# A planner's order of work replaced by a listed one, in a fused attention and MLP kernel

## Chip, core and metric

The kernel runs on one core of a Trainium2 chip. The metric is the device time of one launch in microseconds. Five engines work side by side, each through its own list of instructions in order: TensorE (PE in the profile: matrix products; PEld its weight loads), VectorE (DVE), ScalarE (ACT), GpSimd (POOL) and SyncE (SP), which here issues nearly all DMAs. An instruction whose inputs or whose buffer are not ready holds up all that stand behind it on its engine.

## What is computed

```python
def _attn_ref(q, k, v, g_norm):                      # q, k, v: (8, 8, 576, 64)
    kv = np.einsum('bhsd,bhse->bhde', k, v)
    out = np.einsum('bhsd,bhde->bhse', q, kv)
    rms = np.sqrt(np.mean(out * out, axis=-1, keepdims=True) + 1e-06)
    return (out / rms * g_norm).astype(np.float32)

def _moe_ref(x, w_in, w_out):                        # (4608, 512) (512, 2048) (2048, 512)
    h = x @ w_in
    g = np.maximum(h, 0.0) + np.log1p(np.exp(-np.abs(h)))
    return (g @ w_out).astype(np.float32)
```

Between the two, the attention's output (batch, head, position, 64) is laid out as x, 4608 tokens by 512. Linear attention makes a 64 by 64 matrix kv of each head of a batch; a row of q times it, normed, is a row of x. Then comes an MLP with a softplus. The weights arrive as 64-bit floats, so each is turned to 32 bits on the chip.

## The kernel before

**Precision.** The products are made with 32-bit operands that TensorE rounds. To lose nothing, each operand is split in parts: a rounded high part, and the rest (on ScalarE `high`, on VectorE `low` and `less`). A product is then three passes of parts.

**The stages.** x is worked on in tiles of 128 tokens, 36 in all, tile t from batch t*128 // 576. Before any MLP work:
- `weight(j)`: weight piece j (even: w_in, odd: w_out, of chunk c = j // 2 of 128 hidden units) is loaded (L423, 512 KB), squared for an overflow check on ScalarE (L434, L451), and turned to 32 bits by six operations of VectorE (L438, L442, L447, L455, L460, L464). `split_weight` splits it (L501 or L503, L508 or L511, L514, then on TensorE L525 and L526, L529).
- `kv_of(b)`: k and v of a batch come in four pairs p of 256 KB loads (L685) and a remainder (L683); 16 small products each (L696) add up kv, and ScalarE copies it out (L704).
- `rows(t)`: q of tile t is loaded (L766), transposed on TensorE (L776) and copied by ScalarE (L783); multiplied with kv (L720); squared (L793, ScalarE), summed (L724, VectorE), inverse root (L727 and L728, GpSimd, 2.0 us together), multiplied (L732, VectorE), and transposed (L738). From batch 2 on, q comes by `load_q` and VectorE transposes it (L751).
- `split(t)`: x of the tile is split, L640 on ScalarE, L643 and L646 on VectorE. A block is three tiles, 384 tokens. Its x is also stored (L802, L803) for later use.

**The MLP** has two forms. The first blocks go through `step(s)`: block n times chunk c, `mm1` (12 products, L864), softplus (L886), split (L888 on ScalarE, L875 and L879 on VectorE), and three times `mm2` (3 products each, L871). The first steps are 0 to 3 for block 0 with chunks 0 to 3, then 4 to 7 for block 1, and so on; step 0 needs the three tiles of block 0 split, and weight 0. Later work (`wide_step`, L1066 to L1137) takes 512 tokens at a time and saves products by sums and differences of quarters; it makes up two thirds of the time.

**What sets the order.** None of the functions issues anything: each calls `plan.add(engine, ns, run, after, pos, take, give, ...)`, which appends a task, and `plan.slot(ring)`, which names a buffer to be taken from a ring of buffers. `Plan.order()` then plays the tasks through, with their estimated times `ns`, a model of the DMA's backlog and the positions `pos`, and picks at each point the task that can start first. It also gives each slot its place in its ring. Wherever TensorE would idle for 400 ns by this play (until step 6), it puts in a filler `warm` (L1232): a product of the identity with itself, whose result nobody reads. The result is one list of tasks, and the engines' instructions are issued in its order.

```python
    plan.spare = ("h", warm, 400, mm1s[6][1])
    for t in plan.order():
        t.run()
```

Slots bind engines together: the loads of k and v go through four buffers (`e`), so the load of k's pair 2 has to wait until TensorE has used pair 0. The buffers of weight loads are one for w_in (`raw`) and one for w_out (`rawb`).

## Time and profile before

| | |
|---|---|
| Median of 3 runs | 859.08 us (858.3 to 861.02) |
| The profiled execution | 858.19 us, of it the span of the trace 856.4 us |
| TensorE busy | 843.0 us (98%) |
| VectorE, ScalarE, GpSimd busy | 704.1, 520.6, 76.6 us |
| Fillers (L1232) | 52, from 1.61 to 74.0 us |
| Step 0's first product (L864) | at 44.09 us |
| First output product (L871) | at 58.26 us |
| HBM read, written | 112.98 MB, 52.95 MB |

The span is the time from the first to the last instruction of the trace, and times in the text are counted from its start. In the tables of stretches each engine has its busy time and, in brackets, how many instructions started there; in the timelines a line has the start, the length, the engine, the line of the kernel, and in square brackets how long the engine was idle before and what ended that. A TensorE group's length reaches to the end of its last product's pipeline, so the next group can start before it.

### The profile page before, as it was taken

What the parts mean: (1) busy time and instruction counts of PE and PEld (TensorE: products, weight loads), DVE (VectorE), ACT (ScalarE), POOL (GpSimd) and SP (SyncE); (2) the same over time, 40 slices, a digit from 0 to 9 for tenths busy, and PEclk for the clock granted to TensorE, in tenths of its full rate; (3) what the DMA queues carried; (4) which work ended last, traced back from release to release, by engine and by line L of the source; (5) the groups of instructions that cost most, each with busy time, mean ns of one, the idle gap of its engine ahead of it and who ended that gap; (6) DMA issues with size and microseconds to landing.
All of it is one profiled execution on the core that took longest, in us unless ns stands there. A gap on an engine that the chain in (4) does not pass through costs nothing.

```text
span 856.4 us, 17075 instructions
## 1 busy us (share of the span) xinstructions
PE 843.0 (98%) x6464; PEld 754.1 (88%) x6464; DVE 704.1 (82%) x995; ACT 520.6 (61%) x980; POOL 76.6 (9%) x79
## 2 busy tenths in 40 slices
PE   8899999999999999999999999999999999999998
PEld 5578898999898999999999999998999899999996
DVE  7888898888788889798898788878788766788873
ACT  6766665446344567766667665655868555566654
POOL 0351223111113300000000000000000000000000
PEclk9999999999999999999999999999999999999999
DMA  9998997778884755436644546645364753777864
GB/s 283 297 233 212 261 273 232 185 245 218 214 188 119 194 160 185 142 110 207 210 156 154 180 151 206 195 158 181 124 197 138 234 168 102 240 237 246 249 189 131
DMA packets 239778, 167.07 MB, mean 195 GB/s; under 512 B 106320, under 2 KB 198736, under 8 KB 239696
## 3 DMA queue, kind: packets, MB, share of 16 engines
q1 hardware_dynamic: 239392, 165.86, 65.9%
q8 instruction: 50, 0.82, 0.4%
q14 instruction: 32, 0.26, 0.1%
q10 hardware_dynamic: 304, 0.13, 0.1%
HBM read 112.98 MB, written 52.95 MB: 194 GB/s over the span
## 4 chain that ended last, share of the span: by engine, by line
PE 94%; ACT 1%; DVE 1%; DMA 1%; issue 1%; POOL 0%; SPq 0%; POOLq 0%; DVEq 0%; ACTq 0%
PE banks L1137 31%; PE banks L1066 28%; PE banks L871 16%; PE banks L864 15%; PE banks L720 2%; PE banks L696 2%; DMA loads<-in_k_dram 1%; PE banks L738 0%; PE banks L1232 0%; PE banks L776 0%; DVE units L643 0%; DVE half L732 0%; DVE roots L724 0%; POOL roots L728 0%; ACT w L783 0%
## 5 line engine op out<-in xcount | busy, mean ns | idle before, releaser
L1137 PE MATMUL banks<-pieces,gv 128*128 128x512 f32 x768 | 236.8, 390 | 0.0
L1137 PE MATMUL banks<-pieces,g_False 128*128 128x512 f32 x384 | 149.4, 389 | 0.0
L1137 PEld LDWEIGHTS banks<-pieces,gv 128*128 128x128 f32 x768 | 132.5, 188 | 17.2 <-DVE banks L910 0.2
L864 PE MATMUL banks<-units,pieces 128*128 128x384 f32 x768 | 144.8, 337 | 0.0
L871 PE MATMUL banks<-pieces,gv 128*128 128x512 f32 x576 | 143.3, 393 | 0.0
L864 PEld LDWEIGHTS banks<-units,pieces 128*128 128x128 f32 x768 | 134.7, 188 | 4.5
L871 PEld LDWEIGHTS banks<-pieces,gv 128*128 128x128 f32 x576 | 106.2, 188 | 19.0
L1066 PEld LDWEIGHTS banks<-units,pieces 128*128 128x128 f32 x840 | 111.0, 188 | 6.5 <-ACT banks L1112 0.4
L1066 PE MATMUL banks<-units,pieces 128*128 128x256 f32 x840 | 115.2, 280 | 0.0
L886 ACT ACTIVATE half<-banks 128x384 f32<-128x384 f32 x64 | 31.4, 491 | 94.0 <-PE banks L864 90.7
L1127 DVE TENSOR_TENSOR gv<-g_True,gv 128x1024 fp32r<-128x1024 f32 x47 | 57.5, 1223 | 35.6 <-ACT gv L1124 35.5
L1137 PEld LDWEIGHTS banks<-pieces,g_False 128*128 128x128 f32 x384 | 72.1, 188 | 15.0
L1066 PEld LDWEIGHTS banks<-units,w 128*128 128x128 f32 x504 | 66.7, 188 | 3.7 <-ACT banks L1112 0.2
L1066 PE MATMUL banks<-units,w 128*128 128x256 f32 x504 | 69.6, 280 | 0.0
L728 POOL TENSOR_TENSOR roots<-roots,half 128x8 f32<-128x8 f32 x36 | 62.3, 1731 | 3.0
L1130 DVE SCALAR_TENSOR_TENSOR g_False<-gv 128x1024 fp32r<-128x1024 f32 x47 | 57.6, 1225 | 1.5
L1029 DVE TENSOR_TENSOR units<-loads,units 128x1024 fp32r<-128x1024 f32 x42 | 51.2, 1219 | 6.0 <-ACT units L1026 5.9
L1094 ACT ACTIVATE g_True<-banks 128x256 f32<-128x256 f32 x96 | 36.7, 384 | 30.6 <-PE banks L1066 29.9
L1116 DVE TENSOR_TENSOR g_True<-banks,g_True 128x512 f32<-128x512 f32 x48 | 33.1, 690 | 25.8 <-PE banks L1066 19.8
L931 ACT ACTIVATE m<-banks 128x512 f32<-128x512 f32 x72 | 42.1, 595 | 18.2 <-PE banks L1137 12.5
L1032 DVE SCALAR_TENSOR_TENSOR units<-units 128x1024 fp32r<-128x1024 f32 x42 | 51.4, 1224 | 1.7
L1026 ACT ACTIVATE units<-loads 128x1024 fp32r<-128x1024 f32 x42 | 44.3, 1056 | 12.4 <-PE banks L1066 10.1
(115 smaller groups left out, 1248.7 us busy)
## 6 DMA issues: line engine op xcount, KB each, us to landing
loads<-x SPq DMA_DIRECT2D x180, 128.0 KB, 2.7
part<-m SPq DMA_DIRECT2D x72, 256.0 KB, 3.1
m<-part SPq DMA_DIRECT2D x72, 256.0 KB, 3.4
loads<-form SPq DMA_DIRECT2D x45, 256.0 KB, 3.2
form<-loads SPq DMA_DIRECT2D x36, 256.0 KB, 3.0
raw<-in_moe_w_in_dram SPq DMA_DIRECT2D x16, 512.0 KB, 4.7
loads<-in_k_dram SPq DMA_DIRECT2D x32, 256.0 KB, 4.0
loads<-in_v_dram SPq DMA_DIRECT2D x32, 256.0 KB, 4.5
```

What stands on the lines that cost most here:

```text
L728: nc.gpsimd.tensor_tensor(out=r.tile, in0=r.tile, in1=half, op=ALU.pow)
L864: nc.tensor.matmul(from_the_end(hp, w), lhsT=w_in.tile[:, i, kd * P:(kd + 1) * P], rhs=from_the_end(xv.tile[:, i, kd], w), start=(m == 0), ...
L871: nc.tensor.matmul(mine[i].tile, lhsT=gv.tile[:, m, i * P:(i + 1) * P], rhs=w_out.tile[:, m], start=(c == cs[0] and m == 0), stop=(c == cs ...
L931: a = add("ACT", 690 if ph == LAST else 600, lambda: nc.scalar.activation(new(ot, [P, d_model]), bank.tile, func=AF.Copy, scale=scale if p ...
L1026: nc.scalar.activation(part_of(0, F32R), xl.tile if m > 1 else xl.tile[:, 0], func=AF.Copy, scale=DOWN)
L1029: nc.vector.tensor_tensor(out=part_of(1, F32R), in0=xl.tile if m > 1 else xl.tile[:, 0], in1=part_of(0), op=ALU.subtract)
L1032: nc.vector.scalar_tensor_tensor(out=part_of(2, F32R), in0=part_of(1), scalar=-RADIX, in1=part_of(0), op0=ALU.mult, op1=ALU.add)
L1066: nc.tensor.matmul(from_the_end(place(q), (16, 8)[kd]), lhsT=w[:, m, at:at + P], rhs=from_the_end(dst.tile[:, m, v, kd] if u < 6 else dst. ...
L1094: nc.scalar.activation(dst, src, func=AF.Softplus, scale=1.0 + E)
L1127: nc.vector.tensor_tensor(out=gvt(1, F32R), in0=gt(), in1=gvt(0), op=ALU.subtract)
L1130: nc.vector.scalar_tensor_tensor(out=gt(F32R), in0=gvt(1), scalar=-RADIX, in1=gvt(0), op0=ALU.mult, op1=ALU.add)
L1137: nc.tensor.matmul(from_the_end(mine[i].tile, P), lhsT=(gvt(m, F32R) if m < 2 else gt(F32R))[:, c, i * P:(i + 1) * P], rhs=from_the_end(ou ...
```

## The change

`Plan.order()` no longer plays anything through. It takes two constants: `TURNS`, the order of all tasks, and `HOMES`, the place of each slot in its ring. In `TURNS` a number n from 0 is the n-th task that was added, -1 and -2 are fillers in the first or second bank of ring `h`.

```diff
+TURNS = [
+    -1, -2, -1, -2, -1, -2, -1, -2, 0, 373, 386, 14, 370, 371, 428, 387, -1, -2, -1, -2, -1, -2, -1, -2, -1, -2, -1, 1, 2, 3, 4, 374, 6, 5, 16, 7, 15, 17,
+    28, 388, 372, -2, 18, 376, 429, -1, -2, -1, 382, 20, 21, 430, 8, 19, 375, -2, -1, -2, -1, -2, -1, -2, -1, -2, -1, -2, -1, -2, -1, -2, -1, -2, -1, -2,
...
+]
+
+HOMES = (
...
+)
...
     def slot(self, ring):
-        return Slot(ring)
+        self.slots.append(Slot(ring))
+        return self.slots[-1]
...
-    def order(self):
...
+    def order(self, turns, homes):
+        for s, at in zip(self.slots, homes):
+            s.place = int(at, 36)
+        ring, run = self.spare
+        done = []
+        for n in turns:
+            if n >= 0:
+                done.append(self.tasks[n])
+                continue
+            s = Slot(ring)
+            s.place = -1 - n
+            done.append(Task("PE", 0, lambda s=s: run(s), [], 0.0, [s], [s], 0))
+        assert len(homes) == len(self.slots) and sorted(n for n in turns if n >= 0) == list(range(len(self.tasks)))
+        return done
...
-    plan.spare = ("h", warm, 400, mm1s[6][1])
-    for t in plan.order():
+    plan.spare = ("h", warm)
+    for t in plan.order(TURNS, HOMES):
         t.run()
```

Read against the old order, the list holds the same 3795 tasks. `HOMES` gives every slot that is used the place that it had. The engines' lists differ in their first part only, and are the same from there on:

| engine | tasks in the part that differs, of all | which starts, in the old trace, until |
|---|---|---|
| SP | 73 of 737 | 72 us |
| PE | 234 of 1164, old 207 of 1137: 79 fillers, old 52 | 155 us |
| ACT | 185 of 948 | 162 us |
| DVE | 237 of 989 | 160 us |
| POOL | none of 36 | |

The beginnings, old and new (kv p: the products of pair p of batch 0; W j: weight piece j; q t: q of tile t; r: the remainder of k or v):

| engine | old | new |
|---|---|---|
| SP | W0, k 0, k r, W1, v 0, v 1, k 1, q 0, v r, q 3, W2, k 2, v 2, v 3, W3, k 3, q 1, q 4, k 0 of batch 1, q 4, W4, ... | W0, k 1, q 0, W1, k 0, v 0, q 3, v 1, W2, k 2, k r, k 3, W3, v 3, v 2, v r, q 1, q 4, q 4, W4, ... |
| PE | 13 fillers, kv 0, 2 fillers, kv 1, 1, q 0 transposed, W0 split, 1, q 3, 5, W1 split, 1, kv 2, 6, kv 3, kv r, q 1, W2 split, rows of tile 0, ... | 8 fillers, q 0 transposed, 11 fillers, kv 0, 1, q 3, 3, kv 1, 20 fillers, W0 split, 3, kv 2, kv 3, kv r, 2, rows of tile 0, q 1, W1 split, ... |
| PE, from step 0 on | step 0, x 4, rows 6, W5, q 7, x 5, step 1, kv 0 and 1 of batch 2, rows 7, step 2, x 6, 1 filler, rows 8, W6, L871 of step 0, ... | step 0, rows 6, x 4, step 1, q 7, 1 filler, W5, x 5, rows 7, one L871 of step 0, step 2, x 6, kv 0 and 1 of batch 2, rows 8, two L871 of step 0, ... |

On VectorE the six operations of a weight and the two of a split stood mostly one behind the other; in the new list an operation on something else often stands between two that depend on each other. L438 of W1 stands before L460 of W0, and L508 of W2 right behind L464 of W2. On ScalarE, step 0's L888 stands right behind its L886 (old: seven tasks stand between); L501 of W0 and L434 of W2 stand before L503 of W1; and the first kv copy (L704) stands behind L514 of W0, L451 and L501 of W2 and L434 of W3.

More of the change, by code (lines that the diff above doesn't have):

```diff
@@ L61 @@
 class Plan:
-    HANDOVER = {"PE": 250, "ACT": 120, "DVE": 120, "POOL": 150, "SP": 0}
-    READY = {"PE": 2500, "ACT": 2500, "DVE": 4000, "POOL": 2500, "SP": 700}
-    SWITCH = {("all", "rows"): 90, ("all", "kv"): 90, ("rows", "all"): 250, ("kv", "all"): 250, ("rows", "kv"): 140, ("kv", "rows"): 140}
-    TOGETHER, PATIENCE = 1, 0.0
-    LANDING, FILLED = 3500, 60000
-    KEEP = 4
-    BEGIN = 4000
-    SOON = 150
     def __init__(self, rings, heirs):
@@ L79, in __init__ @@
         self.spare = None
+        self.slots = []
     def slot(self, ring):
-        return Slot(ring)
+        self.slots.append(Slot(ring))
+        return self.slots[-1]
     def add(self, engine, ns, run, after=(), pos=0.0, take=(), give=(), size=0, behind=None, follows=None, kind="all"):
```

117 lines of the change are left out of this document (11 added, 106 removed), and 146 rows, old and new, of the table TURNS.

## The prediction

> **What bounds the kernel now.** I read the page's busy shares and its forty slices first, to find the stages; then the busy time of each engine in stretches of the opening; then the timelines of TensorE (PE), VectorE (DVE) and SyncE (SP) there.
>
> ```profile
> PE 843.0 (98%) x6464; PEld 754.1 (88%) x6464; DVE 704.1 (82%) x995; ACT 520.6 (61%) x980; POOL 76.6 (9%) x79
> ...
> PE   8899999999999999999999999999999999999998
> ```
>
> TensorE is busy 98% of the span, and the slices show where it is not: the first two (43 us) and the last. All that the change moves on TensorE lies before the third tile product of batch 5 (L696) at 155.27 us; from there its list is the old one. So whatever happens, the end moves by as much as that point does.
>
> ```profile
> core 0: us, PE busy (x) PEld busy (x) DVE busy (x) ACT busy (x) POOL busy (x), PEclk, DMA share, GB/s
> 5.00:10.00 5.00, 4.09 (x32) 2.54 (x33) 4.71 (x9) 2.62 (x5) 0.37 (x1) 1.00 1.10 336
> 30.00:40.00 10.00, 8.01 (x149) 5.96 (x143) 8.54 (x15) 8.24 (x17) 4.16 (x4) 1.00 1.01 284
> 40.00:50.00 10.00, 9.16 (x138) 7.57 (x137) 9.29 (x16) 6.34 (x13) 4.11 (x4) 1.00 0.99 236
> 60.00:80.00 20.00, 19.89 (x253) 16.45 (x252) 17.45 (x32) 11.76 (x24) 6.28 (x6) 1.00 0.85 214
> 80.00:155.00 75.00, 75.00 (x746) 67.21 (x745) 67.47 (x117) 44.55 (x87) 19.41 (x18) 1.00 0.89 246
> ```
>
> Until some 40 us the DMA engines are full (share 1.0 to 1.1), VectorE is busy 85 to 94%, and part of TensorE's 80% is filler (L1232: a product nobody reads). After 60 us TensorE has no idle time left. The timeline of TensorE shows the opening:
>
> ```profile
> 1.61 5.92 PE L1232 MATMUL banks<-ident_r 128*128 128x512 f32 x13 [1.61 <-DVE ident_r L1192]
> 8.43 0.69 PE L696 MATMUL banks<-loads 128*64 128x64 f32 x16 [0.91 <-DMA loads<-in_v_dram]
> ...
> 11.18 0.63 PE L776 MATMUL banks<-ident_r,early 128*128 128x128 f32 x4 [0.30 <-DMA early<-in_q_dram]
> ...
> 42.59 1.66 PE L1232 MATMUL banks<-ident_r 128*128 128x512 f32 x6
> 44.09 2.25 PE L864 MATMUL banks<-units,pieces 128*128 128x384 f32 x12
> ...
> 57.06 0.69 PE L720 MATMUL banks<-early,w 64*64 64x64 f32 x32 [0.44 <-ACT w L802]
> ```
>
> The point to watch is 44.09 us, where step 0's first product (L864) starts: real work, then fillers, then the step. Before it lie 20.8 us of real work (34 tasks), some 15 us of fillers and the idle time. After it, up to 155.27, TensorE idles 1.43 us in five gaps and runs 2 fillers.
>
> **The change, part by part.** Durations are from one execution, 858.19 us with a span of 856.4; the sum is made against 858.19. The median of three is 859.08, so 0.9 is added at the end.
>
> *Nothing added or removed but fillers.* The 3795 tasks are the same, and so is the place of every buffer. TensorE gets 79 fillers instead of 52. GpSimd's order is untouched.
>
> *Fillers.* They cost 0.43 us each in the first stretch (2.20, 2.63, 3.06 us and on) and 0.235 after 9 us. A filler is free where TensorE would wait, and paid in full where it would not. In the list 8 come first, 70 between the transposition of q's tile 0 (L776) and step 0, one after. I set the path of TensorE up to step 0 by the starts in the trace: 10 kv products at 0.57, 9 q transpositions at 0.41, 5 weight splits at 0.6, 6 row products at 0.55, 4 x transpositions at 0.4: 17.3; 70 fillers at 0.235 are 16.4, and the first filler of each of 17 groups costs 0.1 more, 1.7. Together 35.4 us. That transposition can start when q's tile 0 lands. Its load goes from eighth on SP to third. There the trace has a load issued at 2.40 and landed at 6.62; q is twice its size, so I take 6.9. Step 0 thus starts at 42.3 at the earliest, and by half a filler (0.12) of left-over gap in each of 17 groups, 2.0, at 44.3. Old: 44.09.
>
> *VectorE up to step 0.* The last input of step 0 is the third part of tile 2 (L646), started at 43.97. A VectorE operation that reads its neighbour's result starts later than one that doesn't:
>
> ```profile
> 28.29 0.69 DVE L643 TENSOR_TENSOR units<-banks,units 128x512 fp32r<-128x512 f32 x1
> 29.02 0.69 DVE L646 SCALAR_TENSOR_TENSOR units<-units 128x512 fp32r<-128x512 f32 x1
> 29.63 0.68 DVE L732 TENSOR_TENSOR half<-banks,roots 128x512 f32<-128x512 f32 x1
> ```
>
> 0.73 us from start to start where the second reads the first, 0.61 where not. Up to that operation the old order has 26 such neighbours and the new one 15: 11 by 0.12, minus 1.3. Two operations fewer stand before it (0.6 each, minus 1.2; the memset L1179 that comes in costs 0.1). The old waits on the way (0.70, 0.19, 0.48, 0.21, 0.99: 2.6) go. New ones come, by position: the first operation on weight 1 (L438) now stands before weight 0's L460, and its load, which landed at 7.63, has 128 KB more ahead of it (q in place of k's remainder) and lands near 8.0: VectorE idle from 7.16, plus 0.85; the residue of weight 1 (L511) waits for ScalarE, which now does a square of weight 2 (L434) first, plus 0.7; that of weight 2 (L508) stands right behind the sum (L464) that ScalarE must read first, 0.85. So 43.97 - 1.2 + 0.1 - 1.3 - 2.6 + 2.4 = 41.4, with as much again of waits unseen (2.6) 44.0. The two paths give 42.3 to 44.3 and 41.4 to 44.0; step 0 waits for both. I take 43.3, 0.8 us earlier, and keep 42.3 to 46.8 (the upper end from the rival with the clock, below).
>
> On chained operations the Trainium skill (VectorE: DVE Perf Modes, The DRAIN you can't avoid) says the opposite of this row: each operation drains anyway, and one can't gain by how they are chained. By it the 1.3 us would not be there, VectorE's path would read 42.7 to 45.3 and the sum some 0.7 more. The rows decide for 0.12 us a pair.
>
> *SyncE and the loads.* All 73 entries that move are loads and stores of the opening; bytes are the same, and the DMA engines are full there, so what comes forward pushes others back. Weight 2 gains about 1.4 us (14.08 to 12.6), but k's pair 2 (L685) needs the buffer that the first kv product (L696) frees. In the old order that was over at 9.12 and the load left at 10.33 unhindered; in the new one 11 fillers and a transposition stand before that product, it ends near 10.9, and everything behind on SP waits: weight 3 leaves at about 13.7 instead of 12.20 and lands near 18.1, old 17.79. Cost on the path: nothing as long as VectorE reaches weight 3 only at 18.4, as its sum above says; up to 1.9 us if that product is later still. What else goes back has room: weight 6 landed at 33.8 and is first read at 41.6, and the x tiles of the stores (L803) are read again no sooner than 65 us.
>
> *ScalarE.* The rounding of step 0's softplus (L888) stood five microseconds behind the softplus (46.38 to 51.44, with splits of later tiles in between); now it follows at once. The first output product (L871) moves before step 2's first product. Worth nothing by itself, since TensorE has other work; it takes away the reasons to idle later. ScalarE's waits (the kv copy L704 stands behind four of weight operations) are inside the 2.6 above.
>
> *After step 0.* From 44.09 to 155.27 the old order takes 111.2 us. With each task at the smallest start-to-start time that its kind, before its next kind, shows in the trace (2.08 for a first product, 0.68 for an output product, 0.47 to 0.58 for kv and rows), the same tasks need 106.8; the new order, with its other neighbours, 106.7. So 4.4 us are to be had, of which 2.7 before 60 us, 1.3 to 80 us, the rest later. I count the part after 80 us as staying, 1.6, and 0.6 of new waits (the first L871 now stands where VectorE's L879 may be about a microsecond late): minus 2.2. Bounds: 4.4, and plus 2 where each early output product waits.
>
> Sum: 858.2 - 0.8 - 2.2 = 855.2; plus 0.9 for the median: **856.1**.
>
> **The rivals.** *A: as before.* The opening is bound by the loads and by VectorE, both full, and the fillers fix step 0 at 44.3; the 4.4 us come back as other waits. For it: DMA share 1.1; 27 fillers more are 6.3 us that can't be skipped. Against it: VectorE's sum without unseen waits ends at 41.4, and the waits of TensorE behind step 0 are on work that the list now brings forward. 858 to 860.5.
>
> *B: slower, by the clock.* The 13 fillers of before ran at 0.427 us each without a break until 7.5 us; those from 9.05 on at 0.235. So TensorE runs at half speed until it has worked for some six microseconds. The new list has 8, over at 5.03, and then a wait for q until 6.9. If the full clock comes only at about 11.3, the 11 fillers that follow cost 0.19 more each, 2.1, and the kv product 0.4 more; k's pair 2 leaves at 12.7, the DMA engines run dry for some 2 us, weight 3 lands at 19.7. All fillers being fixed, nothing catches it up: step 0 at 44.3 + 2.5 = 46.8. If the gain behind it is then lost too: 858.2 + 2.7 + 0.9 = 861.8. It decides from step 0 at 46.7 with nothing gained behind.
> The Trainium skill (TensorE: Matmul & The Clock Gate, Part 1) has this as a rule: a free-running window of about 3.4 us must be busy throughout. By it 8 cold fillers, 3.42 us, hardly ever fill one, and the clock would come between 10.3 and 13.7. The trace agrees that it takes longer than one window (1.61 to at least 6.9 us), and shows no case with a pause.
>
> *C: all of it.* Step 0 at 42.3, and 4 us gained behind: 852.4 + 0.9 = 853.3. Needs no leftover gaps at all.
>
> **How the numbers follow.** About 0.3%, 2.6 us, is what a measurement of this kernel can tell from no change: faster means below 856.5, slower above 861.7. Forecast (854 to 857.5) 0.45, of which 0.36 below 856.5; A 0.22; B 0.25, of which four fifths beyond 861.7, since a late step 0 and waits behind it come together; C 0.08. Faster 0.44, same 0.36, slower 0.20. The range reaches from C's 853.3 to a little beyond B, 862.5; the forecast's own is 854 to 857.5.
>
> **What would show it.** Right: the first L864 between 42.5 and 44; fillers at 0.235 by 8 us; the last L646 before it started before 43.5; the L888 of step 0 within a microsecond of its L886; the kv product that starts TensorE's common part at 152 to 153 instead of 155.27; idle time of TensorE between step 0 and there below 1 us. Wrong: fillers at 0.427 beyond 9 us; SP idle at L685 between 9 and 13 us and a drop in the DMA share there; the first L864 after 45; a wait of more than 1 us before the first L871. A shift of the end that is not the shift of that kv product would contradict the frame of the whole sum.

## The result, and the profile after

The changed kernel takes **867.42 us** (median of six, 864.99 to 869.77), the kernel before 858.58 us beside it (six, 858.30 to 861.02): a ratio of 1.0096, 95% interval 1.0072 to 1.0119. It is 8.8 us slower; 856.1 was forecast, and the range ended at 862.5. The profiled execution took 869.77 us with a span of 868.0, the slowest of its six, so sums against its trace (11.6 us of span) are some 3 us larger than the medians' 8.8.

Lines are now those of the changed kernel: 60 higher than before, so L924 is the first product (L864), L931 the output product (L871), L756 the kv product (L696), L836 the transposition of q (L776), L1292 the filler (L1232), L483 a weight load (L423), L745 a load of k or v (L685). In the experiments' profiles they are 18 or 19 lower than that.

The page's busy line of TensorE and its forty slices, as they were shown of before:

```profile
PE 853.9 (98%) x6491; PEld 761.4 (88%) x6491; DVE 700.2 (81%) x995; ACT 517.7 (60%) x980; POOL 78.2 (9%) x79
...
PE   7899999999999999999999999999999999999998
```

TensorE is busy 10.9 us longer, 98% of the span as before: the share tells nothing. The stretches do, with the columns of before. First the kernel before from 10 to 20 us, then the changed kernel:

```profile
10.00:20.00 10.00, 8.52 (x93) 6.04 (x90) 8.84 (x16) 7.75 (x15) 0.00 (x0) 1.00 1.09 319
```

```profile
5.00:10.00 5.00, 2.24 (x8) 1.69 (x8) 2.45 (x5) 1.60 (x5) 0.25 (x1) 1.00 0.92 287
10.00:20.00 10.00, 10.00 (x65) 7.48 (x64) 5.45 (x10) 4.25 (x10) 0.00 (x0) 1.00 0.65 187
30.00:40.00 10.00, 7.49 (x125) 5.49 (x124) 8.58 (x16) 6.50 (x14) 3.82 (x4) 1.00 1.04 270
40.00:50.00 10.00, 9.78 (x112) 7.57 (x112) 7.00 (x12) 6.25 (x13) 2.99 (x3) 0.83 0.93 212
60.00:80.00 20.00, 19.86 (x255) 17.15 (x256) 16.73 (x31) 12.87 (x27) 6.87 (x5) 1.00 0.84 238
80.00:155.00 75.00, 73.39 (x778) 62.53 (x777) 62.01 (x110) 41.01 (x84) 19.48 (x18) 1.00 0.85 224
```

Three things differ. From 10 to 20 us the DMA share is 0.65 where before had 1.09: the queue of loads stands still, and VectorE has 5.45 us of work instead of 8.84. From 40 to 50 us the clock is 0.83. And behind 80 us, where TensorE had no idle time at all, it loses 1.6 us. The timeline of TensorE shows the opening:

```profile
1.61 3.78 PE L1292 MATMUL banks<-ident_r 128*128 128x512 f32 x8 [1.61 <-DVE ident_r L1252]
8.15 1.08 PE L836 MATMUL banks<-ident_r,early 128*128 128x128 f32 x4 [2.76 <-DMA early<-in_q_dram]
8.88 5.04 PE L1292 MATMUL banks<-ident_r 128*128 128x512 f32 x11
13.86 0.69 PE L756 MATMUL banks<-loads 128*64 128x64 f32 x16
...
23.23 1.15 PE L756 MATMUL banks<-loads 128*64 128x64 f32 x32 [0.57 <-DMA loads<-in_v_dram]
...
40.22 0.38 PE L798 MATMUL banks<-ident_r,half 128*128 128x128 f32 x2 [2.38 <-issue]
...
41.48 2.93 PE L1292 MATMUL banks<-ident_r 128*128 128x512 f32 x6
...
52.07 2.36 PE L924 MATMUL banks<-units,pieces 128*128 128x384 f32 x12
```

The 11 fillers at 8.88 take 0.46 us each, twice the 0.235 of the full clock (the trace has the full clock from 13.89 on; the column PEclk, which reads 1.00 from 5 to 20 us, does not show this), so the first kv product comes at 13.86 instead of 8.43. Step 0 starts at 52.07, 8.0 us later than before.

To follow a loss through a trace I use one measure below, the **lag**: how much later TensorE has finished a given amount of real work (each product group counted at its usual length, fillers not at all) than in the trace of before. In the new kernel it is 9.5 us at 51 us, falls to 5.7 at 100, rises to 11.1 at 170, and stays within half a microsecond of that. So there are two losses: one in the opening, of which 3.8 us are made up behind step 0, and a second of 5.4 between 105 and 170.

Both show the same picture, a queue in order whose head waits. The queue of loads (SPq) in the opening, and ScalarE there:

```profile
10.37 0.37 SPq L483 DMA_DIRECT2D raw<-in_moe_w_in_dram  x1
14.58 0.37 SPq L745 DMA_DIRECT2D loads<-in_k_dram  x1
...
17.24 0.41 SPq L483 DMA_DIRECT2D g<-in_moe_w_out_dram  x1
```

```profile
9.90 0.57 ACT L843 COPY w<-banks 128x512 f32<-128x512 f32 x1
15.45 0.59 ACT L843 COPY w<-banks 128x512 f32<-128x512 f32 x1 [4.97 <-PE banks L836]
```

The load of k's pair 2 (14.58) waits for the first kv product, so weight 3 (17.24) leaves 5.05 us later than before and lands at 21.4 (17.79). ScalarE idles 4.97 us at a copy of q of tile 3, whose transposition stands behind that same kv product; its work for weights 0 and 1 is queued behind, and VectorE idles from 14.08 to 18.46. Little of this reaches TensorE directly before step 0, though. VectorE comes to weight 3 (L498, `g`) only 1.3 us after it has landed, right behind other work:

```profile
22.10 0.69 DVE L520 SCALAR_TENSOR_TENSOR m<-raw,m 128x512 f32<-128x512 uint32 x1
22.71 0.42 DVE L498 TENSOR_SCALAR m<-g 128x512 uint32<-128x512 uint32 x1
```

TensorE waits 0.57 us for the load of v at 23.23, which stands behind weight 3 in the queue, and 0.25 for VectorE at 36.03; from 8.15 to step 0 it idles 3.3 us in all, 2.38 of them in the gap at 40.22 that nothing in the trace releases ("issue").

The second place, the queue of loads and then ScalarE:

```profile
99.02 0.47 SPq L745 DMA_DIRECT2D loads<-in_v_dram  x1
105.05 0.92 SPq L901 DMA_DIRECT2D m<-x  x2
...
108.47 0.88 SPq L483 DMA_DIRECT2D g<-in_moe_w_out_dram  x1
```

```profile
103.91 0.60 ACT L991 ACTIVATE m<-banks 128x512 f32<-128x512 f32 x1 [1.24 <-PE banks L931]
104.40 0.62 ACT L581 ACTIVATE pieces<-m 128x512 fp32r<-128x512 f32 x1
```

The load at 105.05 (x of tile 9, `x_again`) needs a buffer `m` that the third part of weight 8 (`third`, L581) frees. Its input was there at 97.3; it stands behind L991, the copy of an output of step 7. Everything behind that load, weight 9 among it, leaves 11 to 13 us later than before; the loads just ahead of it were some 8.5 us late already, so the hold itself adds some 3 to 5. VectorE then stands at the first operation on weight 9, and step 12's splits stand behind it. VectorE's waits from 98 to 122 us (total, times, longest):

```profile
DVE m L498 <- DMA g<-in_moe_w_out_dram: 3.0, 1, 3.0
DVE gv L935 <- ACT gv L948: 1.6, 3, 1.0
DVE units L703 <- ACT units L700: 1.6, 2, 1.2
```

### The profile page after: what moved, and what is told of

Same layout as the page of the kernel before. It is cut to its first block, busy times and chain, and to the rows that moved or that the text cites. A ratio compares the mean times of both kernels' runs of the same rounds, so it can differ in the third digit from the quotient of the medians.

```text
span 868.0 us, 17114 instructions
## 1 busy us (share of the span) xinstructions
PE 853.9 (98%) x6491; PEld 761.4 (88%) x6491; DVE 700.2 (81%) x995; ACT 517.7 (60%) x980; POOL 78.2 (9%) x79
## 4 chain that ended last, share of the span: by engine, by line
PE 89%; DMA 3%; DVE 3%; ACT 2%; POOL 1%; issue 1%; SPq 1%; DVEq 0%; ACTq 0%
PE banks L1197 30%; PE banks L1126 27%; PE banks L931 13%; PE banks L924 12%; PE banks L780 2%; PE banks L756 2%; PE banks L1292 1%; DMA loads<-in_v_dram 1%; POOL roots L788 1%; DMA g<-in_moe_w_out_dram 1%; DVE half L792 1%; DMA early<-in_q_dram 1%; DMA m<-x 1%; DVE roots L784 1%; PE banks L798 0%
## 5 line engine op out<-in xcount | busy, mean ns | idle before, releaser
L931 PE MATMUL banks<-pieces,gv 128*128 128x512 f32 x576 | 145.9, 395 | 0.7 <-DVE gv L939 0.6
L924 PE MATMUL banks<-units,pieces 128*128 128x384 f32 x768 | 145.3, 337 | 0.5 <-ACT units L700 0.3
L924 PEld LDWEIGHTS banks<-units,pieces 128*128 128x128 f32 x768 | 134.5, 188 | 5.9 <-ACT units L700 0.7
L931 PEld LDWEIGHTS banks<-pieces,gv 128*128 128x128 f32 x576 | 105.5, 188 | 20.9 <-DVE gv L939 1.6
L991 ACT ACTIVATE m<-banks 128x512 f32<-128x512 f32 x72 | 42.2, 596 | 19.2 <-PE banks L1197 12.5
```

The costliest lines, as they stand in the source:

```text
L924: nc.tensor.matmul(from_the_end(hp, w), lhsT=w_in.tile[:, i, kd * P:(kd + 1) * P], rhs=from_the_end(xv.tile[:, i, kd], w), start=(m == 0), ...
L931: nc.tensor.matmul(mine[i].tile, lhsT=gv.tile[:, m, i * P:(i + 1) * P], rhs=w_out.tile[:, m], start=(c == cs[0] and m == 0), stop=(c == cs ...
L991: a = add("ACT", 690 if ph == LAST else 600, lambda: nc.scalar.activation(new(ot, [P, d_model]), bank.tile, func=AF.Copy, scale=scale if p ...
```

## The experiments

All of them compute everything; only the order in the list differs. "Old" and "new" are the orders of the kernels before and after, taken for each engine. Times are medians beside the kernel before on the same chip (858.9 to 859.4 us); step 0 and the lag are from one trace each. Traces of kernels that are alike in the opening differ there: with the old opening by 2.3 us (lag at 100 us: 2.0, 2.0 and -0.3 in e7, e14, e17), and where TensorE's list and the loads are those of the new opening by up to 5 us at step 0 (52.07, 48.23, 49.29 and 46.86 in the changed kernel, e3, e5 and e16) and 1.2 in the lag at 100 us (5.7, 5.0, 5.7 and 4.5). Smaller differences are not read from one.

| run | order | us | ratio, 95% | step 0 | lag at 100, 170 |
|---|---|---|---|---|---|
| changed kernel | new | 867.42 | 1.0072-1.0119 | 52.07 | 5.7, 11.1 |
| e1 | old, 8 first fillers | 859.32 | 0.9995-1.0014 | 44.75 | 0.7, 0.7 |
| e2 | new, 14 + 5 fillers | 867.27 | 1.0081-1.0131 | 46.67 | 2.8, 7.3 |
| e3 | new, W0 before W1 | 868.33 | 1.0095-1.0130 | 48.23 | 5.0, 11.0 |
| e9 | old, all loads new | 868.29 | 1.0092-1.0126 | 50.58 | 9.6, 9.6 |
| e11 | old, first 8 loads new | 861.89 | 1.0021-1.0049 | 47.68 | 3.6, 3.6 |
| e18 | new, all loads old | 881.43 | 1.0239-1.0279 | 57.71 | 17.2, 21.1 |
| e5 | new, W8's third part early | 865.96 | 1.0068-1.0098 | 49.29 | 5.7, 7.9 |
| e7 | old, that part late | 863.99 | 1.0035-1.0082 | 46.03 | 2.0, 6.9 |
| e6 | e5, opening eased | 863.69 | 1.0038-1.0076 | 46.27 | 0.6, 3.4 |
| e12 | e6, W9's load early | 863.40 | 1.0036-1.0070 | 45.24 | 1.2, 3.6 |
| e17 | old, new from step 8 | 863.96 | 1.0039-1.0080 | 43.78 | -0.3, 3.9 |
| e16 | new, old from step 8 | 866.44 | 1.0067-1.0101 | 46.86 | 4.5, 8.5 |
| e8 | old, VectorE woven | 859.83 | 1.0005-1.0025 | 45.03 | 1.0, 1.0 |

### The clock and VectorE's head: e1, e2, e3

```diff
 TensorE, e1 (old):  13 fillers, kv pair 0, ...
-13 x filler
+ 8 x filler
 TensorE, e2 (new):
- 8 x filler, transpose q tile 0, 11 x filler, kv pair 0
+14 x filler, transpose q tile 0,  5 x filler, kv pair 0
 VectorE, e3 (new):
+L520 of W0
 L498 of W1
-L520 of W0
```

> The old order with one edit: 8 fillers ahead of the first kv product instead of 13, as in the new list. Theory 1 (the clock starts it, the list's blocked queues make it dear): TensorE pauses from 5.0 to about 8.4 us, the full clock comes some 3 us later than in the old trace, but nothing waits behind a cold stretch of fillers, so step 0 starts at most 1.5 us later and the time is 858.5 to 860.5. Rival 2 (the half clock alone is the price): step 0 at 48 or later, 862 or more.

> The new list with 14 fillers in front of q's transposition instead of 8, and 5 behind it instead of 11: as many in all, but no pause. Theory 1: full clock by 8 to 9 us (13.9 in the new trace), first kv product at 10.5 instead of 13.9, k's pair 2 leaves at 11.3 instead of 14.6, step 0 near 48.5 instead of 52.1, time 863 to 865. Rival 3 (the order of the lists itself, whatever the clock): step 0 after 50.5, time 866 to 868.

> The new list with one task moved: on VectorE, the product of weight 0 (L460) stands before the first operation on weight 1 (L438) again, as in the old order, so the buffer of weight 0 is free at about 7.5 us instead of 10.3 and weight 2's load leaves then. Theory 1: k's pair 2 still waits for the first kv product, so the time falls by less than 0.8 us: 866.5 to 867.5. Rival 3: weight 2 and all behind it come 2 us sooner, 865 or less.

In e1 the full clock came only at 13.4 us (7.83 before), and the time did not move. Its TensorE timeline:

```profile
1.61 3.78 PE L1273 MATMUL banks<-ident_r 128*128 128x512 f32 x8 [1.61 <-DVE ident_r L1233]
8.24 1.12 PE L737 MATMUL banks<-loads 128*64 128x64 f32 x16 [2.86 <-DMA loads<-in_v_dram]
```

The kv product waits for its load and starts at 8.24 either way. Half a clock costs nothing here, where TensorE is ahead of its inputs; in the new kernel 11 fixed fillers at that clock stand ahead of the product that frees the buffer. With them moved to the front (e2) the full clock came at 6.6, that product at 10.29, k's pair 2 left at 11.02 and step 0 came 5.4 us earlier than in the changed kernel, though no earlier than in e16 (46.86), which has its opening untouched; the lag of 2.8 at 100 us does lie outside the 4.5 to 5.7 of those kernels. But the median did not move (863 to 865 expected), though its own trace was 3.9 us shorter than that of the new kernel. e3 gained nothing (868.33; 866.5 to 867.5 expected). So neither of these alone gives the 8.8 us back.

### Loads and lists come in pairs: e9, e11, e18

```diff
 e9:  TensorE, ScalarE, VectorE old
-     loads and stores old
+     loads and stores new
 e11: all old, but the head of the loads
+     W0, k of pair 1, q 0, W1, k and v of pair 0, q 3, v of pair 1, then the old order
 e18: TensorE, ScalarE, VectorE new
-     loads and stores new
+     loads and stores old
```

> One part of the change alone: the queue of loads and stores in the new order, and TensorE, ScalarE, VectorE with all their old lists. Theory 1 (the order of the loads costs little; the losses come from where the compute lists put their waits): first kv product at 8.5 to 10, q's transposition where it was, k pair 2 leaves at 10.5 to 11.5, step 0 at 44 to 46, time 858.5 to 861. Theory 2 (the new order of loads is itself the loss: remainders and later keys leave 7 to 12 us later by the list): step 0 at 48 or later and a time of 863 to 868.

> The old lists, and of the loads only the first eight in the new order (W0, the second v of pair 1, q of tile 0, W1, the k of pair 0, q of tile 3, the first v of pair 1); behind them the loads and stores in their old order. With all loads in the new order the lag was 4.0 us at 31 us and 9.6 at 91. Theory 1 (the head of the queue starts it: k of pair 0 leaves 2.1 us later, the clock falls back to half while TensorE waits, and the rest of the order adds its own part): first kv product 10 to 11, lag 2 to 4 at 31 us and not over 5 at 91 us, time 860.5 to 863.5. Theory 2 (the head is the whole loss, what comes later follows from it): lag 7 us or more at 91 us and a time of 866 to 869. Theory 3 (the head costs nothing, all of it lies in the later order): 858.5 to 860.

(What this record calls the second v of pair 1 is its k.)

> The new lists of TensorE, ScalarE and VectorE, ranked against each other as in the new list, and all loads and stores in the old order. Theory 1 (loads and compute lists fit only in pairs): q of tile 0 lands at 10.5 to 11.5, the first kv product comes at 15.5 to 18, k pair 2 leaves behind it, step 0 at 52 to 57, time 866 to 874. Theory 2 (the new order of loads is the loss and the compute lists are no worse than the old): 857.5 to 861. Theory 3 (the order between the engines plays no part): 890 or more, as when they were ranked by the old list.

The loads alone cost as much as the whole change (868.29, just above the second theory's 868, with step 0 at 50.58 as that theory has it), the compute lists alone 22.5 us, beyond the first theory's 874. In e9 and in e18 TensorE's timelines say why:

```profile
4.76 2.38 PE L1273 MATMUL banks<-ident_r 128*128 128x512 f32 x6
10.49 1.12 PE L737 MATMUL banks<-loads 128*64 128x64 f32 x16 [3.35 <-DMA loads<-in_v_dram]
```

```profile
11.19 1.09 PE L818 MATMUL banks<-ident_r,early 128*128 128x128 f32 x4 [5.80 <-DMA early<-in_q_dram]
11.93 4.62 PE L1274 MATMUL banks<-ident_r 128*128 128x512 f32 x11
16.48 0.69 PE L738 MATMUL banks<-loads 128*64 128x64 f32 x16
```

Each waits for the tile that the other order would have brought first. In e9 the queue of loads waits for products of kv 9.3 us in all from 8 to 92 us (3.2 in before, 7.2 in the changed kernel): the k and v buffers come free by the old list while the loads stand in the new order. The first eight loads are worth 2.9 us of its 9 (e11), with the lag at 3.6 from 50 us to the end; the rest is the later order. The new kernel's time is therefore not the sum of a bad part and a good one: the lists are fitted to the loads, and the pair is still slower.

### The second loss: e5, e7

```diff
 ScalarE, e5 (new):
+L581 of W8
 L561 of W10, L862 of tile 11, ..., L991 of step 7
-L581 of W8
 ScalarE, e7 (old):
-third part of W8
 ...
 third part of W10
+third part of W8
```

> The new list with one instruction moved: in ScalarE's list the third part of weight block W8 (third(), L581 of the new kernel, at 104.40 in its trace) goes to the place right ahead of the first part of W10 (L561, 100.00). Theory 1, a buffer in front of a queue: the loss between 110 and 170 us (lag of TensorE's done work against before 5.7 to 11.1 us) begins in the queue of loads, which stands still from 99.5 to 105.0 because its head, the load of tile 9 for x_again (L901), wants the m buffer that this third part frees, and the third part stands in ScalarE's list behind a copy (L991) that waits for a product of step 7. Expected by it: that load leaves within 1 us of the load before it, at 99.5 to 100.5, not 105.05; W9's load (L483, 108.5) leaves at 102.5 to 104; VectorE does not wait 3.0 us at L498 at 111.2; the lag at 170 us is 5.5 to 7.5, and the time 862 to 864.5. Theory 2, the later stalls are TensorE's own list (it puts the first product of step 12 ahead of the rows of tile 14): the queue flows, but the lag still rises by 4 us or more after 110, and the time stays at 866.5 to 868.5.

> The converse: the old list with one instruction moved, the same third part of W8 (L581 here, at 84.66 in the trace of before) to the place in ScalarE's list behind the third part of W10 (97.39). Theory 1: the queue of loads stands still from 91 to 98.0 for the m buffer, all loads behind it leave 6 to 7 us late (W9's at 102 to 104, not 96.7), VectorE waits at W9's first instruction, and TensorE loses 2 to 5 us between 105 and 165: time 860.5 to 863.5. Theory 2 (it is TensorE's list): the old order of TensorE hides it, and the time stays 858 to 859.5.

One instruction moved. The queues of loads of e5 and of e7:

```profile
98.66 0.47 SPq L727 DMA_DIRECT2D loads<-in_v_dram  x1
99.23 0.96 SPq L883 DMA_DIRECT2D m<-x  x2
...
104.36 1.34 SPq L988 DMA_DIRECT2D part<-m  x2
105.75 0.42 SPq L465 DMA_DIRECT2D g<-in_moe_w_out_dram  x1
```

```profile
94.18 0.47 SPq L726 DMA_DIRECT2D loads<-in_v_dram  x1
100.51 0.92 SPq L882 DMA_DIRECT2D m<-x  x2
...
103.89 0.99 SPq L464 DMA_DIRECT2D g<-in_moe_w_out_dram  x1
```

In e5 the load leaves at once (99.23), VectorE's wait of 3.0 us is gone, and the rise of the lag from 105 to 170 falls from 5.4 to 2.3. The time gains 1.5 us by the medians (the intervals overlap) and misses its range of 862 to 864.5: the queue stands again, from 101.4 to 104.4, at a store of step 7 that waits for L991, so weight 9 leaves at 105.75 and not by 104. In e7 the good order, given only this delay, loses 4.6 us by the median (860.5 to 863.5 was expected); its lag, 2.0 before the moved instruction matters, jumps to 6.9 between 100 and 130, and TensorE there waits:

```profile
PE banks L737 <- DMA loads<-in_v_dram: 2.6, 2, 2.4
PE banks L761 <- ACT early L745: 1.4, 1, 1.4
```

So the traces show the hold in both directions, and the time shows it for e7: one ScalarE operation of 0.6 us, placed late, holds the queue of loads. That goes with some 3 us of the second loss here, by the lag of one trace each (1.5 by the medians), and with 4.6 us of time in the old order.

### Both eased: e6, e12

```diff
 e6 = e5, and
 TensorE: 14 fillers ahead of q's transposition, 5 behind
 VectorE: L520 of W0 ahead of L498 of W1
 ScalarE: L843 of tile 3 behind L563 of W1
 e12 = e6, and
 loads: L483 of W9 ahead of the stores of step 7
```

> The new list with the third part of W8 moved as in the run before, and the opening eased in three places: 14 fillers ahead of the first transposition of q and 5 behind it (not 8 and 11), VectorE's L520 of W0 ahead of its L498 of W1, and ScalarE's copy of the turned q of tile 3 (L843) behind W1's L563. Theory 1 (the two losses are separate and both are blocked queues): first kv product at 10.0 to 10.6, k pair 2 leaves by 11.3, ScalarE idle before W1's squares' sums gone, step 0 at 45 to 47, lag 1.5 to 3 at 90 us and 2 to 4.5 at 170, time 859.5 to 862. Theory 2 (the opening's delay is made good by the slack behind step 0 whatever its size): the opening is earlier but the time is that of the run before within 1 us, 862 to 865.

> The new list with the eased opening and the third part of W8 moved (863.69 us), and with W9's load (L483) put ahead of the first of three stores of step 7 (L1007) that stand in front of it in the queue of loads; there the queue stood from 96.6 to 99.35 for the copy (L991) that the store takes. Theory 1: W9 leaves at 96.5 to 97.5 and not at 100.75, VectorE's first instruction of W9 runs at 103 to 105 (105.98), TensorE's lag rises by at most 1.5 us from 110 to 170 (2.5 before it), time 861.5 to 863.5. Theory 2 (what is left of the late loss is the order of TensorE's own list around steps 12 and 18): W9 is early and the lag still rises by 2.3 us or more; time 863 to 864.5.

e6 regains 2.3 us more by the median than e5, with the lag at 0.6 at 100 us. Its 863.69 lies above the first theory's range and inside the second's, but not within 1 us of e5, as the second has it; first product (10.38), pair 2 (11.11), step 0 (46.27) and the lag at 170 us (3.4) are the first theory's; the lag at 90 us, 0.7, is better than its 1.5 to 3. So the opening's loss is not simply made good behind step 0. In e12 weight 9 leaves at 97.19, as meant, and nothing comes of it: VectorE's first operation on it runs at 106.56 (105.98 in e6) and the lag still rises by 2.2 us from 110 to 170, nearly the second theory's 2.3. The rest of the second loss lies in the compute lists, or in another held load. In e5, where the lag still rises by 2.3 us, 0.57 of it is idle time of TensorE and the larger part is dearer products: 1.2 us by output products (L931), 0.5 by the products of the rows. That points at TensorE's own list.

### Which stretch: e17, e16

```diff
 e17: every engine old up to step 8's first output product (some 101 us)
+     then new
 e16: every engine new up to there
+     then old
```

> The old lists up to the first second-half product of step 8 and the new ones behind it, the engines ranked as in the list that each part comes from. Theory 1 (the new lists behind step 8 cost by themselves, some 2 us, apart from the late third part of W8 that is early here): lag 0 to 2 at 100 us, a rise of 1.5 to 3.5 us from there to 170, time 860.5 to 863.5. Theory 2 (they are harmless when loads and third part are early): the lag stays level within 1 us, time 858 to 860.5.

> The new lists up to the first second-half product of step 8 and the old lists behind it, by engine as in the run before of that kind, but with the engines ranked against each other as the new list has them up to there, and as the old list behind. Theory 1 (two losses that add): step 0 at 49 to 52, lag 5 to 7 us at 100, level behind it within 1.5 us, time 862 to 864.5. Theory 2 (the late loss is the opening's delay coming out): the lag rises by 3 us or more behind 105 and the time is 866 to 869. Theory 3 (the order between the engines plays no part): stalls of 3 and 5.8 us in step 0 and step 2 as before, time over 878.

In e17 nothing is late at 100 us (lag -0.3), the third part of W8 is early, and the new lists behind step 8 still cost: lag 4.0 by 160, 5.0 us by the median (3.3 to 6.9; 863.96 is half a microsecond above the first theory's range). Its queue of loads:

```profile
95.79 0.67 SPq L464 DMA_DIRECT2D g<-in_moe_w_out_dram  x1
103.68 0.32 SPq L987 DMA_DIRECT2D part<-m  x1
105.07 0.98 SPq L659 DMA_DIRECT2D early<-in_q_dram  x2
106.16 0.77 SPq L882 DMA_DIRECT2D m<-x  x1
```

It stands 7.1 us at a store of step 7: the copy it takes ran at 103.06 on ScalarE, behind the softplus of step 10 (102.26), which the new lists put ahead of it. The load of x of tile 11 leaves at 106.16 (100.67 before), and ScalarE waits 3.42 us for it. That this is the price of the new tail was not tried. Of the 4.3 us that e17 loses between the first products of steps 8 and 26, TensorE idles 1.8; the other 2.5 are again dearer products, 1.55 of them output products. In e16 the opening costs less than in the changed kernel (step 0 at 46.86, lag 4.5 at 100), then the lag rises by 4.0. Those are the second theory's numbers, but the rise is for the most part in two stalls of TensorE, 2.07 us at 104.57 and 1.52 at 118.45, where the two orders meet: at the first, TensorE's new head has step 10's first product early, and ScalarE (L928) has not yet read the bank that it takes; at the second TensorE waits for VectorE (L774). So e16 gives no price for the opening alone.

### Chained neighbours on VectorE: e8

The numbers are those of the tasks; seven pairs of neighbours are taken apart.

```diff
 VectorE (old), between 24 and 42 us:
-58 59 52 393 60 62 63 396 397 407 64 72 73 66 433 410 ...
+58 52 59 393 60 62 396 63 397 407 72 64 73 66 410 433 ...
```

> The old lists, with VectorE's stretch from 24 to 42 us woven so that 22 instead of 29 of the neighbours up to step 0 take what the one before them made; same instructions, same loads, same other lists. The prediction priced each such pair at 0.12 us. Theory 1 (VectorE's path sets step 0): 7 pairs less are 0.84 us, of which what lies behind VectorE's waits at 37.8 and 38.7 us (2 pairs, 0.2 us) surely counts: the last split before step 0 at 43.2 to 43.8 (43.96), time 858 to 859. Theory 2 (VectorE waits for others at 38.7 to 39.6 whatever it saved before): step 0 stays at 43.9 to 44.2, time the same within 0.3 us of before.

The pairs taken apart start 0.60 us after one another (28.80 to 29.40, 34.46 to 35.05), 0.73 where chained in the rows of before: the price held. The time did not: 859.83, slower by 0.05 to 0.25%. VectorE's own timeline has waits of 0.86, 0.69, 0.68 and 1.04 us in the stretch, for ScalarE's copies and GpSimd's roots, which can swallow it. No gain came, as the second theory has it, but neither of its numbers was met: step 0 at 45.03 is 0.8 beyond its range, and the time is 0.84 us above the kernel before beside it, where 0.3 was expected.

### One list for all engines: e4, e10, e13, e14, e15

These were to split the change by stretch or by part: e4 and e14 old up to step 0 or step 8 and new behind it, e15 and e13 the new or the eased head with the old tail, e10 the new lists with old loads. The engines were ranked against each other by the old list wherever that was possible. No expectation on a stretch or a part could be judged by them.

```diff
 e10, e15, e14: each engine's own list as in e18, e16, e17
-               ranked as in the list each part comes from
+               ranked as in the old list
```

> The old order of every engine until step 0 (on TensorE until its first product, on ScalarE until its softplus, on VectorE until its first split), and the new order of what remains; SyncE's order is the old one throughout. Step 0 at 44.1 us. If the gain behind step 0 is the new order's own (in the new trace the lag falls from 9.5 us at step 0 to 5.3 us at 86 us): 854 to 856. If the 5.7 us that the new trace loses between 115 and 166 us are that order's own too: 859 to 861. If both gain and loss come only from being late: 858 to 859.

> The other half of the split: the loads and stores in their old order, and TensorE, ScalarE and VectorE with the new lists. Theory 1 (loads and compute lists only fit together as pairs): q of tile 0 lands at 10.8 to 11.5 as before, and TensorE's new list has its transposition first, so the first kv product comes at 16 to 18, k pair 2 leaves behind it at 16.5 to 18.5, step 0 at 52 to 56, and the time is 868 to 874. Theory 2 (the new order of loads is the loss by itself, and the new compute lists are no worse than the old ones): the time is 857.5 to 861.

> The new lists with the eased opening up to the first second-half product of step 8 (some 101 us), and the old lists of every engine behind it. Theory 1 (what is left of the late loss, 2.2 us from 110 to 170, lies in the order of the compute lists behind step 8): the lag stays level from 110 us on, within 0.5 us, TensorE's stall inside step 18 (0.9 us) is gone, time 860 to 862. Theory 2 (it is the late start of the loads and weights before step 8 that comes out there, whatever the order behind): the lag rises by 1.5 us or more after 110 and the time stays at 863 to 864.5.

> The old lists up to the first second-half product of step 8, and the new lists of every engine behind it (the third part of W8 is early, as in the old list). Theory 1 (the order behind step 8 costs by itself): step 0 at 44 to 45, lag 0 to 1 at 100 us, then a rise of 1.5 to 3 us by 170, with TensorE waiting in step 11, 12 or 18: time 860 to 862. Theory 2 (the new order behind step 8 is harmless when the loads are early): the lag stays level and the time is 858 to 859.5.

> The new lists of the changed kernel, opening as it is, up to the first second-half product of step 8, and the old lists behind it (the third part of W8 then stands ahead of the copy that held it). Theory 1 (two losses that add): lag 5 to 7 us at 100 as in the changed kernel, level behind it within 1 us, time 862 to 864.5, so that 3 to 5.4 of the 8.4 us belong to the lists behind step 8 and the rest to the opening. Theory 2 (the late loss is the opening's delay coming out): the time stays at 866 to 868.

They took 874.93, 894.23, 881.73, 868.23 and 881.89 us, and answer another question. e10, e14 and e15 have, engine by engine, the same lists as e18, e17 and e16, and are slower by 12.8, 4.3 and 15.5 us. VectorE in e15, and in e16, at the last split that step 0 needs (in e15 for its later products):

```profile
53.87 0.69 DVE L685 TENSOR_TENSOR units<-banks,units 128x512 fp32r<-128x512 f32 x1 [2.94 <-ACT w L844]
```

```profile
45.70 0.68 DVE L685 TENSOR_TENSOR units<-banks,units 128x512 fp32r<-128x512 f32 x1
```

L685 (VectorE) and the copy L844 (ScalarE) only read the same bank of PSUM. Where the copy stands first in the one list, the split waits for it: 8.6 us in four waits from 40 to 70 us in e15, none in e16. The list is thus not only an order for each engine. e4 was built the same way, and its loss is not split here into order and rank.

## Why the prediction was wrong

**The frame held.** The common kv product came at 166.37, 11.1 us later than 155.27; the span grew by 11.6.

**The opening: the step that failed is the price of the fixed fillers on TensorE's path.** The sum had 70 of them at 0.235 us, 16.4, and 1.7 for the first of each group. From start to start:

| | forecast | measured |
|---|---|---|
| q's transposition starts | 6.9 | 8.15 |
| real work from there to step 0 | 17.3 | 18.5 |
| 70 fillers | 18.1 | 22.1 |
| idle time of TensorE (forecast: half of the 2.0 of left-over gaps) | 1.0 | 3.3 |
| step 0 starts | 43.3 | 52.07 |

The four differences, 1.25, 1.2, 4.0 and 2.3, are the 8.8 us by which step 0 was missed. The fillers' 4.0 are those at half clock: the 11 behind q's transposition took 5.04 us and not 2.6, six at 41.48 took 2.93 and not 1.41. Of the idle time 2.38 us is one gap ("issue") that no term of the sum held. The sum was right that a fixed filler is paid in full, and wrong in the clock at which it is paid. The same TensorE list gave 21.1, 20.3 and 19.9 us of fillers with 1.0, 3.2 and 1.1 of idle time in e3, e5 and e16, and step 0 at 48.23, 49.29 and 46.86: fillers and gaps make most of the spread there, and the trace of the changed kernel has the most of both.

Wrong as forecasts too were SyncE's words "cost on the path: nothing as long as VectorE reaches weight 3 only at 18.4", "up to 1.9 us if that product is later still", and for ScalarE "inside the 2.6 above". Measured: the kv product ended at 14.54 and not near 10.9; weight 3 left at 17.24 and not at 13.7, and landed at 21.4 and not near 18.1. ScalarE's 4.97 us at the copy of q was not in the sum at all, though the new list shows the copy there: I had costed what each moved instruction waits for, not what stands behind it. In this trace these waits held TensorE itself for only 0.8 us before step 0. VectorE's path was nearly as late, all the same (its last split for step 0 started at 51.56), and where step 0 came earlier with the same lists, TensorE waits for VectorE's splits behind it, 2.49 us in e16, 1.66 in e3 and 2.44 in e5:

```profile
56.15 0.66 PE L780 MATMUL banks<-ident_r,half 128*128 128x128 f32 x4 [2.49 <-DVE units L685]
```

So TensorE's path set step 0, with VectorE's close behind it; how the two share what the opening costs in the end, no run splits.

**Fillers.** 0.235 by 8 us was wrong; full clock at 13.9.

**VectorE.** The path of 41.4 to 44.0 became 51.56 for its last split. The 0.12 us a pair are right and worth nothing (e8), because the stretch was not bound by VectorE's own work; that term of 1.3 was a saving on an engine that waits. Weight 1 landed at 9.24 (8.0 forecast).

**ScalarE's rounding** of step 0 (L948) followed its softplus within 0.5 us, as forecast.

**Behind step 0.** Minus 2.2 was forecast, between minus 4.4 and plus 2; it took 114.3 us where the old order took 111.2, plus 3.1. Two terms failed. The first is the gain. Of the 111.2 us before, 1.43 were idle and 109.7 work, and the sum had the work fall towards 106.7. It did not fall in any trace with the whole new list: 112.0 in the changed kernel, 110.8 to 113.7 in e2, e3, e5, e6 and e12. The lag did fall by 3.8 us from 51 to 100 us in the changed kernel, but with the same lists and an earlier step 0 it did not (4.7 to 5.0 in e3, 5.3 to 5.6 in e5, 2.5 to 4.4 in e16), so that fall is a late step 0 made up, and no gain of the order is shown. (The sum also slips in itself: of 4.4 us with 2.7 before 60 us and 1.3 to 80, 0.4 is left after 80 us and not 1.6; with 0.4 it would have read minus 3.4, farther off.) The second term is "0.6 of new waits": 5.4 us came from 105 to 170 us, 2.2 of idle time and 3.1 of dearer products. Some 3 of the 5.4 go with one late ScalarE operation in front of the queue of loads (e5, e7); the rest comes with the new order behind step 8 (e17: 5.0 us by itself in a kernel with an early opening), for the larger part as dearer products. An output product takes 0.228 us from start to start among output and first products, but 0.32 to 0.34 right ahead of or right behind the small products of kv and the rows, in the kernel before as well. Between the first products of steps 8 and 26 TensorE's new list has 17 such places, the old one 8, e17 14. That comes to 1.0 of the 2.0 us by which output products are dearer there in the changed kernel (0.9 of 1.2 in e5, 0.6 of 1.55 in e17); most of the rest stands right behind waits. This is read from the traces; no run changed TensorE's list alone there.

**The rivals.** B had the direction and the chain of the opening (product late, k's pair 2 at 12.7, weight 3 landed at 19.7), and was too small: 14.58 and 21.4, and it priced the opening at 46.8. Its cause was not enough, either: half clock alone costs nothing where TensorE waits for its loads (e1), and giving the clock back (e2) did not change the median; on the fixed fillers of the new opening it is the 4.0 us above, where B had 2.1 and 0.4. What the Trainium skill (TensorE: Matmul & The Clock Gate, Part 1) says, a window of about 3.4 us that must be busy throughout, fits: with 8 fillers and the pause the lasting full clock came at 13.9, 13.4 and 12.6 (changed kernel, e1, e5), in e5 after a first stretch of it from 5.8 to 9.2 that the pause ended; with 14 fillers it came at 6.6 and stayed (e2). Its other rule, that chaining on VectorE makes no difference (VectorE: DVE Perf Modes, The DRAIN you can't avoid), does not fit the 0.73 against 0.60 us here; for the time it would have been the better guide. A and C were not seen.

**What stays open.** Which part of the 8.8 us the opening has in a typical execution: single traces say 5.7 at 100 us, e6 with its eased opening regains 2.3. The last 4.4 us of e6 and e12 are in part the lag's rise behind 110 us (2.2 in e12); the more frequent changes between output products and small ones on TensorE there, and the store that holds the loads in e17, are candidates that were not tried. No version ran faster than the kernel before. In that kernel VectorE waits 1.4 us from 20 to 60 us for copies that read the same bank (L643 for L802); ranking the splits first was not tried.

## What to carry to other kernels

When instructions move in an in-order queue, list for each what now stands behind it, and for each load which instruction frees its buffer and what stands in front of that on its own engine: more than half of the second loss goes with a queue of loads held by a short operation on another engine. A filler that a list fixes on an engine with no time to spare is paid in full, at the clock of that moment. An order of loads and an order of compute are one thing: each half of this change alone was as bad as the whole, or worse (868.29 and 881.43 us). Where one list serves several engines, the order between engines can bind as well as the order on each.

## What the hardware showed beyond that

- TensorE's clock falls and returns in steps: after the first full clock, every half-clock stretch in the traces lasted 3.4 us or a multiple (41.2 to 44.6 in the changed kernel after the gap of 2.38 us; 10.0 to 16.8 in e9; 49.3 to 59.5 in e10).
- The gap of 2.38 us at 37.84 has no releaser. A fetch of instructions (16 KB) stands in the DMA queues there, with the DMA share at 1.04; before had 1.08 us at 34.7 with a fetch, and e6 2.12 us at the same task. Other runs (e3, e7, e16) have such a fetch without a gap. That the fetch is the cause is argued, not shown.
